# Scaling a normalised block one pass later, and decoding late weights one pass earlier, in a fused delta-rule and gMLP kernel

## The chip, the cores and the metric

The kernel runs on one core of one Trainium2 chip. The metric is the device time of one execution in microseconds (us), lower is better. TensorE is called PE in the profile, VectorE DVE, ScalarE ACT, GpSimd POOL and SyncE SP; SP and POOL issue most of the DMAs here. About 0.5% is what a measurement of this kernel can tell from no change.

## The reference

First a linear-attention recurrence with the delta rule over 768 steps, for 4 batches of 8 heads with a head size of 48; then, on its output, a gated MLP whose gate mixes the tokens of a batch.

```python
for t in range(S):                              # k_n: k with each row divided by its length
    y[:, :, t] = einsum('bhd,bhde->bhe', q[:, :, t], state)
    v_old = einsum('bhde,bhd->bhe', state, kt)
    state = state + bt * einsum('bhd,bhe->bhde', kt, vt - v_old)

h = gelu(x @ w_in)                              # x: y, heads side by side, 384 wide; h: 1024 wide
u, v = h[..., :512], h[..., 512:]
v_n = (v - mean(v)) / sqrt(var(v) + 1e-6) * g_ln
v_s = einsum('ts,bsd->btd', w_sg, v_n) + b_sg[None, :, None]
out = x + (u * v_s) @ w_out
```

## The kernel before, in words

The 768 steps are cut into 12 chunks of 64. The loop over `c` runs 14 passes: in pass c it does chunk c of the recurrence and, as `Ffn(c - 2)`, the first half of the MLP (up to `u` and `v`) for the chunk that ended two passes before. I call the pass by its c. Passes 12 and 13 have MLP work alone. What is left, the mixing of tokens (`spatial`) and the projection (`project`), is the tail, and starts when all chunks are done.

A pass is written as a list of steps, and on every engine the instructions of the loop stand in that order. `turn` transposes the 64 rows of `x` of both batch pairs on PE (L672); ACT copies them, rounded, into `xh` (L673), and DVE subtracts to get the rest, `xl` (L677). A product of two float32 matrices is made of three matmuls with such high and low parts (`mm3`, L650 to L652). `own` and `old` make the chunk's updates, `state` carries the state on, `read` gives the output, and beside them run Gram matmuls for a chunk five passes ahead (passes 0 to 6); all of these are small matmuls of L73. `corner` fills in a part of a triangular inverse for the next chunk: `corner_b` ends with an ACT copy into `z` (L460), which the matmuls beside `read` need. `value` and `gate` are the MLP's matmuls, each closed by an ACT activation (L688 and L720).

`moments` (DVE, L692 and L693) takes mean and variance of `v`. `norm` puts 12 tiny DVE instructions (two columns each: reciprocal square root by Newton steps, L700 to L703) on a list called `slow`, from which `tick` takes one at a time between the larger DVE steps of the inverse (list `bg`), and which `flush` empties. `scale` empties the list and then scales both blocks `vg` on ACT (L711); it is called at the end of the pass, so on ACT it stands between the last copies of this pass and `xh` of the next. `ustore` writes the blocks to memory from POOL's queue in the next pass.

`w_out` and `w_sg` are only needed in the tail. They come in 20 pieces: eight of `w_out`, which are decoded from their stored words in three parts (DVE, then ACT's cast L600, DVE and POOL, then DVE), and twelve of `w_sg`, which are split in two (ACT's cast and a DVE subtraction, L655 and L656). Six buffers `raw` take them as they land; SP issues the load of a piece as soon as its buffer is free. `unit()` stands in seven places of a pass and does one round: part three of one piece, part two of the next, part one of the one after. The pool of these buffers lies where the recurrence's `low` and `prep` pools were, and is opened after pass 9, so rounds run from pass 10 on.

The tail's instructions are written after the loop, and a scheduler places them among the loop's last ones. Its first part loads `vD`, the scaled blocks, into three buffers `vraw` (L1018), from which ACT and DVE make `vnh` and `vnl` (L655 and L656 again).

Of the kernel before, what the change touches and what calls it, by code (L numbers as in the profile page):

```python
# [22 lines left out]
NCH = SEQ // T  # L23
# [15 lines left out]
AHEAD = 5  # L39
# [6 lines left out]
def delta_rule_gmlp_kernel(  # L46
# [14 lines left out]
    nc = tc.nc  # L61
# [93 lines left out]
    bg, slow = [], []  # L155
# [10 lines left out]
    def flush():  # L166
        while slow:
            slow.pop(0)()
# [489 lines left out]
    class Ffn:  # L658
# [46 lines left out]
            self.rs, self.mr = rs, mr  # L705

        def scale(self):
            flush()
            for bi in range(2):
                vg = self.vg[bi]  # L710
                nc.scalar.activation(  # L711
                    out=vg, in_=vg, func=AF.Identity, scale=self.rs[:, bi:bi + 1], bias=self.mr[:, bi:bi + 1])
# [120 lines left out]

    END = {1: (0, "end"), 2: (2, "end"), 3: (4, "end"), 4: (6, "end"), 5: (8, "end")}
    BEGIN = {2: (1, "own"), 3: (3, "own"), 4: (5, "own"), 5: (7, "own")}
    units, stores = [], []
    for c in range(NCH + 2):
        ffn = Ffn(c - 2) if c >= 2 else None
        ch = chain(c) if c < NCH else None
# [6 lines left out]
        def feeds(name, *i):  # L846
            if ffn:
                getattr(ffn, name)(*i)
                if name in COST:
                    spent(name)  # L850
# [6 lines left out]
        def unit():  # L857
            if units:
                units.pop(0)()
# [41 lines left out]
        tload(c + 2)  # L901
        qload(c + 2)
        at("own")
        feeds("value", 0)
        unit()
        does("old0")
        feeds("moments", 0)
        feeds("gate", 0)
        does("old1")
        while stores:  # L910
            stores.pop(0)()
        unit()
        feeds("value", 1)
        does("state0")
        unit()
        feeds("moments", 1)
        feeds("norm")
        feeds("gate", 1)
        at("corner")
        corner(corner_a)  # L920
        does("state1")
        unit()
        if ch:
            gstore(c + AHEAD, nc.sync)
        norms_next()
        feeds("gate", 2)
        unit()
        corner(corner_b)
        feeds("gate", 3)
        unit()  # L930
        if c + AHEAD < NCH and (c + AHEAD) % 2 == 1:
            zload((c + AHEAD) // 2)
        does("read0")
        does("read1")
        at("end")
        unit()
        if ffn:
            ffn.scale()
            stores.append(ffn.ustore)
        if ch:  # L940
            stores.append(lambda c=c: xstore(c))
        if c == NCH - 3:
            prep_ctx.close()
            wpool = ctx.enter_context(tc.tile_pool(name="wpool", bufs=1, side="left", reuse_waits="tile"))
            wouth = wpool.tile([P, ND, DM], F32R, name="wouth")
            woutl = wpool.tile([P, ND, DM], F32R, name="woutl")
            wsgh = wpool.tile([P, NT, SEQ], F32R, name="wsgh")
            wsgl = wpool.tile([P, NT, SEQ], F32R, name="wsgl")
            half = DM // 2
            raws = {}  # L950
            n_w = 2 * (ND + NT)

            def w_fetch(k):
                if k >= n_w:
                    return
                raws[k] = raw = wpool.tile([P, half, 2], I32, name="raw", bufs=6)
                if k < 2 * ND:
                    nc.sync.dma_start(
                        out=raw, in_=words(w_out)[:, k // 2, half * (k % 2):half * (k % 2) + half])
                else:  # L960
                    st, c0 = (k - 2 * ND) // 2, DM * (k % 2)
                    nc.sync.dma_start(
                        out=raw.bitcast(F32).rearrange("p n x -> p (n x)"),
                        in_=w_sgT[st * P:st * P + P, c0:c0 + DM])

            def w_parts(k):

                if k >= n_w:
                    return [lambda: None] * 3
                raw = raws.pop(k)  # L970
                if k < 2 * ND:
                    f = wpool.tile([P, half], I32, name="f", bufs=3)
                    m = wpool.tile([P, half], I32, name="m", bufs=3)
                    cols = slice(half * (k % 2), half * (k % 2) + half)
                    return decode(raw, f, m, wouth[:, k // 2, cols], woutl[:, k // 2, cols])
                st, c0 = (k - 2 * ND) // 2, DM * (k % 2)
                rawf = raw.bitcast(F32).rearrange("p n x -> p (n x)")
                return [lambda: split(wsgh[:, st, c0:c0 + DM], wsgl[:, st, c0:c0 + DM], rawf)] + [lambda: None] * 2

            ahead = []  # L980

            def w_unit(k):
                if k >= 2:
                    ahead[k - 2][2]()
                if k >= 1:
                    ahead[k - 1][1]()
                ahead.append(w_parts(k))
                ahead[k][0]()
                w_fetch(k + 4)

            for k in range(4):
                w_fetch(k)
            units = [lambda k=k: w_unit(k) for k in range(n_w + 2)]
    while units:
        units.pop(0)()
    while stores:
        stores.pop(0)()
    by_hand.close()
# [117 lines left out]
```

## Time and profile before

| | before |
|---|---|
| median of 3 runs | 578.78 us (577.52 to 579.75) |
| the profiled execution, its own time | 572.28 us |
| its span, first to last instruction | 570.6 us |
| PE busy | 462.1 us (81%) |
| DVE busy | 363.9 us (64%) |
| ACT busy | 216.2 us (38%) |
| POOL busy | 98.1 us (17%) |
| mean granted clock of PE | 0.895 |

A row of the timeline gives start and length in us, engine, line, operation, out<-in with sizes, how many were merged, and in brackets the idle time of the engine just before and what ended it. Chains give start, length, engine, tile and line. In a row of the view by stage each engine has its busy time and count, then come the granted clock, the DMA share and GB/s. A busy PE is not PE at its peak, and "issue" is time in which PE waited for nothing that the profile shows. The passes open with their transposes (L672): pass 9 at 307.5 us, 10 at 333.5, 11 at 355.2, 12 at 379.1 and 13 at 399.4; the tail's matmuls begin at 416.7.

### The profile page before, as it was taken

The page shows a single profiled execution, that of the slowest core. Times are in us where ns is not written, and L with a number is a line of the kernel's source. Part 1 is how long each engine was busy: PE and PEld are TensorE (multiplying, and loading weights), DVE is VectorE, ACT ScalarE, POOL GpSimd, SP SyncE. Part 2 cuts the span into 40 slices and gives each one's busy share as a digit, 9 for nine tenths or more (in the row PEclk, how much of TensorE's full clock was granted, in tenths as well). Part 3 has the DMA queues.
Part 4 walks back from the last instruction along what each step waited for, and adds up shares of the span by engine and source line. Part 5 has one row for each costly group of instructions (what it writes and reads, how often), then busy time and mean ns, then how long its engine had stood idle before and what let it go on. Part 6 is the DMA issues. An engine that isn't in the chain of part 4 may idle for free.

```text
span 570.6 us, 18229 instructions
## 1 busy us (share of the span) xinstructions
PE 462.1 (81%) x7635; PEld 416.5 (73%) x7635; DVE 363.9 (64%) x1273; ACT 216.2 (38%) x482; POOL 98.1 (17%) x157
## 2 busy tenths in 40 slices
PE   7244588469796987797998979666599999999997
PEld 5233377357685876686877868556499999999997
DVE  1999799999699649664994338645346545333332
ACT  2212147243763663465547446245343213110110
POOL 3310001320021020102010122301115122211220
PEclk9758858678997987898999999797799999999999
DMA  8798997993699569656954942378449664452113
GB/s 185 171 283 167 214 181 170 184 250 115 121 235 223 199 112 231 163 186 123 257 187 79 266 151 86 107 189 245 140 157 221 168 173 124 118 139 84 43 41 125
DMA packets 153218, 94.35 MB, mean 165 GB/s; under 512 B 117712, under 2 KB 138832, under 8 KB 152176
## 3 DMA queue, kind: packets, MB, share of 16 engines
q1 hardware_dynamic: 137008, 68.84, 51.8%
q0 software_dynamic: 6336, 21.50, 10.5%
q10 hardware_dynamic: 9792, 2.85, 2.8%
q8 instruction: 60, 0.98, 0.8%
q14 instruction: 22, 0.18, 0.1%
HBM read 59.08 MB, written 34.08 MB: 163 GB/s over the span
## 4 chain that ended last, share of the span: by engine, by line
PE 63%; DMA 14%; DVE 9%; issue 5%; ACT 5%; SPq 2%; ACTq 1%; DVEq 0%
PE ps L73 18%; PE ps L650 16%; PE ps L652 14%; PE ps L651 14%; DMA kd<-kqT 3%; DMA vraw<-vD 3%; DMA gd<-gk 2%; DMA z<-zD 2%; DMA zl<-gd 2%; SPq L300 1%; DMA ztd<-zt 1%; ACT vg L711 1%; DMA zD<-zl 1%; DMA kt<-ktok 1%; DVE winl L608 1%
## 5 line engine op out<-in xcount | busy, mean ns | idle before, releaser
L73 PE MATMUL ps<-kd 48*64 48x128 f32 (+1 forms) x896 | 59.7, 292 | 22.7 <-DMA kd<-kqT 20.4
L73 PEld LDWEIGHTS ps<-kd 48*64 48x64 f32 x896 | 52.0, 159 | 25.0 <-issue 20.4
L650 PE MATMUL ps<-winh,xh 128*128 128x512 f32 x72 | 35.4, 491 | 24.9 <-ACT xh L673 20.7
L356 DVE TENSOR_TENSOR ztmp<-zl 128x72 f32<-128x72 f32 (+13 forms) x228 | 52.0, 263 | 1.5
L363 DVE TENSOR_TENSOR zl<-zl,ztmp 128x72 f32<-128x72 f32 (+13 forms) x228 | 50.9, 261 | 0.0
L655 ACT CAST gh<-ga 128x384 fp32r<-128x384 f32 x32 | 16.4, 514 | 90.6 <-POOL ga L1042 90.6
L1042 POOL TENSOR_TENSOR ga<-ga,uT 128x384 f32<-128x384 f32 x32 | 33.7, 1057 | 98.8 <-DVE ga L1040 79.7
L677 DVE TENSOR_TENSOR xl<-ps,xh 128x384 fp32r<-128x384 f32 x24 | 12.3, 552 | 54.8 <-ACT xh L673 54.7
L650 PE MATMUL ps<-xh,winh 128*128 128x256 f32 x144 | 44.5, 309 | 0.0
L73 PE MATMUL ps<-v,z 64*64 64x48 f32 x768 | 31.6, 238 | 14.9 <-issue 14.0
L73 PEld LDWEIGHTS ps<-v,z 64*64 64x64 f32 x768 | 28.6, 153 | 18.7 <-issue 17.3
L651 PE MATMUL ps<-xl,winh 128*128 128x256 f32 x144 | 40.6, 282 | 0.0
L652 PE MATMUL ps<-xh,winl 128*128 128x256 f32 x144 | 40.5, 282 | 0.0
L688 ACT ACTIVATE vg<-ps 128x512 f32<-128x512 f32 x24 | 14.3, 597 | 69.1 <-PE ps L652 67.3
L656 DVE TENSOR_TENSOR gl<-ga,gh 128x384 fp32r<-128x384 f32 x32 | 19.1, 596 | 32.4 <-ACT gh L655 32.4
L515 POOL MEMSET flag<- 1x1 f32 x22 | 2.0, 90 | 218.9 <-PE ps L73 218.9
L650 PEld LDWEIGHTS ps<-winh,xh 128*128 128x128 f32 x72 | 16.0, 222 | 29.7 <-ACT xh L673 21.3
L73 PE MATMUL ps<-s,qo 48*64 48x48 f32 x704 | 27.8, 232 | 6.8 <-issue 6.8
L283 ACT COPY gk<-ps 128x256 f32<-128x256 f32 x40 | 15.0, 376 | 46.0 <-PE ps L73 34.0
L651 PE MATMUL ps<-winl,xh 128*128 128x512 f32 x72 | 32.4, 450 | 0.0
L652 PE MATMUL ps<-wouth,gl 128*128 128x384 f32 x96 | 32.3, 336 | 0.0
L652 PE MATMUL ps<-winh,xl 128*128 128x512 f32 x72 | 32.3, 448 | 0.0
(141 smaller groups left out, 1369.8 us busy)
## 6 DMA issues: line engine op xcount, KB each, us to landing
kd<-kqT SPq DMA_DIRECT2D x20, 384.0 KB, 7.8
vD<-vg POOLq DMA_DIRECT2D x24, 256.0 KB, 4.2
uD<-ut POOLq DMA_DIRECT2D x12, 512.0 KB, 5.7
vraw<-vD SPq DMA_DIRECT2D x48, 128.0 KB, 2.8
uT<-uD SPq DMA_DIRECT2D x32, 192.0 KB, 4.0
gd<-gk SPq DMA_DIRECT2D x11, 512.0 KB, 4.9
z<-zD SPq DMA_DIRECT2D x22, 256.0 KB, 5.5
v<-vtok SPq DMA_DIRECT2D x12, 384.0 KB, 5.4
```

The costliest lines, as they stand in the source:

```text
L73: return nc.tensor.matmul(out=out, lhsT=lhsT, rhs=rhs, start=start, stop=stop, skip_group_check=True)
L283: nc.scalar.copy(out=GK[c % N_M][:, i, :, qd // 2], in_=st["ps"][:, :, 0].rearrange("p j (h t) -> p j h t", h=2))
L356: tv.tensor_tensor(out=st["tmp"][:, at:at + (r1 - r0) * w].rearrange("p (r t) -> p r t", t=w), in0=z[:, r0:r1, i:i + 1].broadcast_to([P, r ...
L363: tv.tensor_tensor(out=z[:, r0:r1, i + 1:32], in0=z[:, r0:r1, i + 1:32], in1=st["tmp"][:, at:at + (r1 - r0) * w].rearrange("p (r t) -> p r ...
L650: nc.tensor.matmul(out=ps, lhsT=sh, rhs=mh, start=(first and i == 0), stop=False)
L651: nc.tensor.matmul(out=ps, lhsT=sh, rhs=ml, start=False, stop=False)
L652: nc.tensor.matmul(out=ps, lhsT=sl, rhs=mh, start=False, stop=(last and i == n - 1))
L655: nc.scalar.copy(out=hi, in_=src)
L656: nc.vector.tensor_tensor(out=lo, in0=src, in1=hi.bitcast(F32), op=ALU.subtract)
L677: nc.vector.tensor_tensor(out=self.xl[:, :, bi], in0=srcs[bi], in1=self.xh[:, :, bi].bitcast(F32), op=ALU.subtract)
L688: nc.scalar.activation(out=vg, in_=ps, func=AF.Gelu_apprx_tanh)
L1042: nc.gpsimd.tensor_tensor(out=ga, in0=ga, in1=uT[:, d], op=ALU.mult)
```

## The change

Three things are written in another order; no instruction of the computation is added or removed.

First, `scale` no longer empties `slow`, and is not called at the end of its pass: it is put on a list `scales`, which the next pass empties behind its first `value`. Second, `slow` is emptied at the end of the pass as before, and also ahead of the unit behind `gate` 2 if `bg` is empty. Third, the block that closes `prep_ctx`, opens `wpool` and defines the pieces moves from the end of pass 9 to before its first `value`, with three empty rounds ahead, so that the first four rounds fall in the second half of pass 9.

```diff
         def scale(self):
-            flush()
             for bi in range(2):
                 vg = self.vg[bi]
                 nc.scalar.activation(
...
-    units, stores = [], []
+    units, stores, scales = [], [], []
     for c in range(NCH + 2):
...
         at("own")
+        if c == NCH - 3:
+            prep_ctx.close()
+            wpool = ctx.enter_context(tc.tile_pool(name="wpool", bufs=1, side="left", reuse_waits="tile"))
...
+            def w_unit(k):
+                if k >= 2:
+                    ahead[k - 2][2]()
+                if k >= 1:
+                    ahead[k - 1][1]()
+                ahead.append(w_parts(k))
+                ahead[k][0]()
+                w_fetch(k + 4)
+
+            for k in range(4):
+                w_fetch(k)
+            units = [lambda: None] * 3 + [lambda k=k: w_unit(k) for k in range(n_w + 2)]
         feeds("value", 0)
+        while scales:
+            scales.pop(0)()
         unit()
...
         feeds("gate", 2)
+        if not bg:
+            flush()
         unit()
...
         at("end")
         unit()
         if ffn:
-            ffn.scale()
+            flush()
+            scales.append(ffn.scale)
             stores.append(ffn.ustore)
...
-        if c == NCH - 3:
-            prep_ctx.close()
...
-            units = [lambda k=k: w_unit(k) for k in range(n_w + 2)]
     while units:
         units.pop(0)()
+    while scales:
+        scales.pop(0)()
     while stores:
         stores.pop(0)()
```

How this moves instructions on ACT and SP is seen in three places. The first is ACT at the end of pass 9 and the start of pass 10, from the last activation of `gate` (`ut`). Before:

```order
L460 COPY z_106<-ps 32x8x2x32 x2
L720 ACTIVATE ut<-ps 128x256
L563 COPY x_5273<-ps 128x384
L478 COPY w_108<-ps 128x512
L563 COPY x_5309<-ps 128x384
L478 COPY w_108<-ps 128x512
L711 ACTIVATE vg<-vg,mr,rsq_y 128x512 x2
L673 CAST xh<-ps 128x3x128 x2
L688 ACTIVATE vg<-ps 128x512
```

And with the change:

```order
L600 CAST wouth<-f 128x192
L460 COPY z_106<-ps 32x8x2x32 x2
L719 ACTIVATE ut<-ps 128x256
L600 CAST wouth<-f 128x192
L563 COPY x_5336<-ps 128x384
L478 COPY w_108<-ps 128x512
L563 COPY x_5372<-ps 128x384
L478 COPY w_108<-ps 128x512
L600 CAST wouth<-f 128x192
L673 CAST xh<-ps 128x3x128 x2
L688 ACTIVATE vg<-ps 128x512
L710 ACTIVATE vg<-vg,mr,rsq_y 128x512 x2
```

Three casts of `w_out` pieces now stand here, one of them ahead of the copy into `z`, and the scaling has gone behind the activation of `value`.

The second place is ACT at the start of pass 12, behind the last copies of the recurrence (`x`). Before:

```order
L563 COPY x_6079<-ps 128x384
L655 CAST wsgh<-raw 128x384
L655 CAST vnh<-vraw 128x512
L711 ACTIVATE vg<-vg,mr,rsq_y 128x512 x2
L673 CAST xh<-ps 128x3x128 x2
L655 CAST vnh<-vraw 128x512 x3
L688 ACTIVATE vg<-ps 128x512
```

And with the change:

```order
L563 COPY x_6105<-ps 128x384
L655 CAST wsgh<-raw 128x384
L673 CAST xh<-ps 128x3x128 x2
L655 CAST vnh<-vraw 128x512
L688 ACTIVATE vg<-ps 128x512
L710 ACTIVATE vg<-vg,mr,rsq_y 128x512 x2
L655 CAST wsgh<-raw 128x384
```

The first cast of the tail (`vnh`) and the scaling stood ahead of `xh`, and are now behind it.

The third place is SP's queue, from the first piece's load to the tail's first loads. Before:

```order
L958 DMA raw<-w_out 128x384 x8
L962 DMA raw<-w_sgT 128x384 x11
L1003 DMA g_sb<-g_ln 128x4x1
L1004 DMA bsg_bc<-b_sg 128x768
L1018 DMA vraw<-vD_75 64x512
L962 DMA raw<-w_sgT 128x384
L1018 DMA vraw<-vD_75 64x512 x5
```

And with the change:

```order
L919 DMA raw<-w_out 128x384 x8
L923 DMA raw<-w_sgT 128x384 x12
L1009 DMA g_sb<-g_ln 128x4x1
L1010 DMA bsg_bc<-b_sg 128x768
L1024 DMA vraw<-vD_75 64x512 x6
```

One load of `w_sg` has moved ahead of the tail's loads, and nothing else.

More of the change, by code (lines that the diff above doesn't have):

```diff
@@ L903, in delta_rule_gmlp_kernel @@
         at("own")
[L904 to L937, printed above, removed]
-            ffn.scale()
-            stores.append(ffn.ustore)
-        if ch:
-            stores.append(lambda c=c: xstore(c))
         if c == NCH - 3:
@@ L992, in delta_rule_gmlp_kernel @@
                 w_fetch(k)
-            units = [lambda k=k: w_unit(k) for k in range(n_w + 2)]
+            units = [lambda: None] * 3 + [lambda k=k: w_unit(k) for k in range(n_w + 2)]
+        feeds("value", 0)
+        while scales:
+            scales.pop(0)()
+        unit()
+        does("old0")
+        feeds("moments", 0)
+        feeds("gate", 0)
+        does("old1")
+        while stores:
+            stores.pop(0)()
+        unit()
+        feeds("value", 1)
+        does("state0")
+        unit()
+        feeds("moments", 1)
+        feeds("norm")
+        feeds("gate", 1)
+        at("corner")
+        corner(corner_a)
+        does("state1")
+        unit()
+        if ch:
+            gstore(c + AHEAD, nc.sync)
+        norms_next()
+        feeds("gate", 2)
+        if not bg:
+            flush()
+        unit()
+        corner(corner_b)
+        feeds("gate", 3)
+        unit()
+        if c + AHEAD < NCH and (c + AHEAD) % 2 == 1:
+            zload((c + AHEAD) // 2)
+        does("read0")
+        does("read1")
+        at("end")
+        unit()
+        if ffn:
+            flush()
+            scales.append(ffn.scale)
+            stores.append(ffn.ustore)
+        if ch:
+            stores.append(lambda c=c: xstore(c))
     while units:
         units.pop(0)()
+    while scales:
+        scales.pop(0)()
     while stores:
```

## The prediction

> **What bounds the kernel now.** I read the chain of waits first, in order of time; its last lines are these (start, length, what).
>
> ```profile
> 363.62 0.80 PE ps L650
> ...
> 381.31 5.58 DMA vraw<-vD
> 386.97 0.63 ACT vnh L655
> ...
> 405.67 0.80 ACT vg L711
> 406.89 0.79 PE ps L650
> ```
>
> From 406.89 us on the chain is TensorE alone. Three times before that, TensorE's first `value` matmul (L650) comes behind a ScalarE instruction that it does not need: the scaling of the previous blocks (L711) or a cast for the tail (`vnh`). I call these matmuls V11, V12 and V13, after the passes c = 11, 12, 13, and the transposes that open a pass T11, T12, T13. The view by stage has the reads that end pass 10, then a row from each T to its V, and for two of them the matmuls behind (stretch, length, busy time and count of PE, PEld, DVE, ACT, POOL, then granted clock, DMA share, GB/s):
>
> ```profile
> 352.80:355.20 2.40, 2.40 (x132) 2.20 (x131) 2.19 (x8) 1.95 (x5) 0.53 (x1) 1.00 0.30 85
> 355.20:363.62 8.42, 3.20 (x137) 2.78 (x135) 5.76 (x26) 3.28 (x8) 1.55 (x4) 0.92 0.19 51
> 363.62:367.00 3.38, 3.38 (x8) 2.71 (x9) 3.17 (x10) 0.32 (x1) 1.01 (x2) 0.50 0.15 40
> 379.13:389.42 10.29, 0.88 (x10) 0.64 (x6) 3.12 (x15) 3.34 (x7) 0.68 (x2) 0.67 0.76 182
> 389.42:393.00 3.58, 3.58 (x9) 2.83 (x10) 2.21 (x4) 1.64 (x4) 2.02 (x4) 0.51 0.90 305
> 399.41:406.89 7.48, 0.82 (x9) 0.58 (x7) 3.68 (x16) 3.92 (x9) 0.66 (x2) 0.75 0.13 38
> 430.00:566.80 136.80, 136.76 (x789) 136.44 (x787) 59.32 (x102) 23.33 (x45) 33.68 (x32) 1.00 0.48 125
> ```
>
> T12 to V12 is 10.29 us with 0.88 us of matmuls, T13 to V13 7.48 with 0.82. After the first two waits the clock is about 0.50 for some 3.4 us, so a cooling costs 3.4 x 0.5 = 1.7 us more; I take the third alike. The last row is the tail: no gap, full clock. So whatever brings V13 forward comes off the end. The timeline of ScalarE and the waits say what is late:
>
> ```profile
> 361.69 1.52 ACT L711 ACTIVATE vg<-vg,mr,rsq_y 128x512 f32<-128x512 f32 x2 [4.65 <-DVE mr L703]
> 379.62 0.51 ACT L655 CAST wsgh<-raw 128x384 fp32r<-128x384 f32 x1
> 386.97 0.62 ACT L655 CAST vnh<-vraw 128x512 fp32r<-128x512 f32 x1 [6.83 <-DMA vraw<-vD]
> ACT wouth L600 <- DVE f L596: 0.9, 2, 0.5
> ```
>
> **The end of the recurrence, T12 to the tail.** The change takes L711 out from between T and `xh`, and in the new order pass 12's `xh` stands ahead of the first `vnh`. What then lies between T12 and V12 is one weight cast (379.62 + 0.51 = 380.13), `xh` and the split behind it: about 1.7 us for 10.29, gain 8.6. At T13 four `vnh` casts still stand ahead of `xh`; the fourth needs a load whose buffer the first frees. When do these loads start?
>
> ```profile
> 374.06 0.60 ACT L688 ACTIVATE vg<-ps 128x512 f32<-128x512 f32 x1 [1.12 <-PE ps L652]
> 378.06 0.56 DVE L656 TENSOR_TENSOR wsgl<-raw,wsgh 128x384 fp32r<-128x384 f32 x1 [0.50 <-ACT wsgh L655]
> 379.02 0.43 SPq L1003 DMA_DIRECT2D g_sb<-g_ln  x1
> ```
>
> SP's queue holds its last weight loads until a `raw` buffer comes free, that is until the piece six before is split (378.62, then `g_sb` at once). Afterwards the split that frees the last of them follows the second `value` of pass 11, whose activation (374.06) now lies 10.4 us behind V11, 8.7 without the cooling; with cast and split some 10 us. So `vraw` starts some 11 us behind V11 (near 375) and lands by 381 at the 5.6 us of the chain's row. The first `vnh` then ends by 382, as the matmuls of `value` in pass 12 do, and the fourth by 386 to 389, around T13. I take 2.0 us from T13 to V13 (1.7 if it is there, 3.5 if not): gain 5.5. Three coolings less: 3 x 1.7 = 5.1. Sum **19.2 us**, if V11 stays where it is.
>
> **Passes 9 to 11: the cost.** Eight pieces of `w_out` are decoded in 2.70 us of VectorE each (from one L590 to the next below). Now they start in pass 9, where VectorE stood idle for 11.56 us.
>
> ```profile
> 336.32 1.02 DVE L677 TENSOR_TENSOR xl<-ps,xh 128x384 fp32r<-128x384 f32 x2 [11.56 <-ACT xh L673]
> 339.27 0.25 DVE L590 TENSOR_SCALAR m<-raw 128x192 int32<-128x192 int32 x1
> 352.45 0.25 DVE L590 TENSOR_SCALAR m<-raw 128x192 int32<-128x192 int32 x1
> 355.15 0.25 DVE L590 TENSOR_SCALAR m<-raw 128x192 int32<-128x192 int32 x1
> 359.27 0.16 DVE L700 TENSOR_SCALAR ve<-mv 128x2 f32<-128x2 f32 x1
> 361.43 0.16 DVE L703 SCALAR_TENSOR_TENSOR mr<-mv,rsq_y 128x2 f32<-128x2 f32 x1
> L958 SPq DMA_DIRECT2D raw<-w_out x1: 420/420/420, 323.8 to 323.8; - x1
> DMA to landing us min/median/max: 5.4/5.4/5.4
> 327.18 1.18 ACT L460 COPY z<-ps 32x512 f32<-32x512 f32 x2 [0.64 <-PE ps L73]
> 333.08 0.26 PE L73 MATMUL ps<-u,m 64*64 64x48 f32 x2 [2.83 <-issue]
> 356.68 0.35 ACT L600 CAST wouth<-f 128x192 fp32r<-128x192 f32 x1 [0.49 <-DVE f L596]
> ```
>
> SP's order is unchanged, so opening the pool sooner loads nothing sooner: the first piece lands at 323.8 + 5.4 = 329.2. ScalarE's first cast (L600) now stands ahead of the `z` copy L460, and needs VectorE's first part of that piece (about 1.5 us): 330.7, so the copy ends near 332.2 instead of 328.36, and behind it wait `x`, `w` and TensorE's reads. Of these 3.8 us, 2.83 lie over the stall at 333.08 that is there now ("issue"): T10 about 1 us late. VectorE goes on: norm 2.3 (359.27 to 361.59), then up to the fourth piece three rounds less a last part, 3 x 2.7 - 0.7 = 7.4; so 329.2 + 1.5 + 2.3 + 7.4 = 340.4, and with a split of 0.55 V10 is at 341.0. Now it ends an `xl` pair begun at 336.32 and V10 is at 337.66: **3.3 us late**. In pass 10 VectorE has `xl`, `v`, `m` (336.32 to 339.27: 2.95), four rounds (10.8) and two moments (1.8): 356.0 for the eighth piece. Its cast, one weight cast and the `z` copy again stand in line: 0.35 + 0.51 + 1.18 give 358.0. Reads take 2.4 (352.80:355.20), and T11 to the end of `own` 3.76 (8.42 less the wait of 4.66 named below): V11 at 358.0 + 2.4 + 3.8 = 364.2 against 363.62. So V11 is **0.6 us late** in place of being earlier: the wait for `mr` at 361.69 is gone, and the same VectorE work has been paid before. Bounds: 3 us earlier (TensorE alone from V10, were it not late), 5 us later (each of the two `z` copies and V10 lets TensorE cool, 3 x 1.7).
>
> ```profile
> 363.62 0.80 PE L650 MATMUL ps<-winh,xh 128*128 128x512 f32 x1 [4.66 <-ACT xh L673]
> 238.00 0.26 PE L73 MATMUL ps<-v,z 64*64 64x48 f32 x2 [3.24 <-issue]
> 239.46 0.79 PE L650 MATMUL ps<-winh,xh 128*128 128x512 f32 x1
> ```
>
> A wait of 3.24 us was already followed by slow matmuls (0.79, as at 363.62). The new waits before V10 and at the copy are of 3.6 and 3.8 us; at V10 the loss of 1.7 mostly hides behind VectorE, which sets the next `z` copy, so I add nothing. The Trainium skill speaks against the change here: "TensorE: Matmul & The Clock Gate", section "What's actually happening", says that about 3.4 us without work, in a window that runs freely, brings half clock, and as long a busy stretch restores it. By it both new waits may cool: my time plus up to 3.4 us. The trace agrees on half clock and the 3.4 us; that 3.24 us sufficed, a free window allows.
>
> **Passes 3 to 9: small terms.** L711 also leaves its place ahead of `xh` here, and goes ahead of the copies behind `value`.
>
> ```profile
> 155.57 0.49 PE L650 MATMUL ps<-winh,xh 128*128 128x512 f32 x1 [0.69 <-DVE xl L677]
> 207.38 0.51 PE L650 MATMUL ps<-winh,xh 128*128 128x512 f32 x1 [0.99 <-DVE xl L677]
> 265.58 0.50 PE L650 MATMUL ps<-winh,xh 128*128 128x512 f32 x1 [0.66 <-DVE xl L677]
> 312.82 0.50 PE L650 MATMUL ps<-winh,xh 128*128 128x512 f32 x1 [0.51 <-DVE xl L677]
> 187.23 0.37 ACT L283 COPY gk<-ps 128x256 f32<-128x256 f32 x1 [0.45 <-PE ps L73]
> 187.50 0.38 ACT L285 COPY m<-ps 128x256 f32<-128x256 f32 x1
> 188.44 1.06 PE ps L73 x32
> ```
>
> Gain: four waits for `xl`, 2.85 us. Loss: in the four passes with Gram work (3 to 6) the copy of `m` ends at 187.88, 0.56 us before the next matmuls at 188.44; two scalings (1.52) less the idle 0.45 push it 1.07, so 0.5 past, four times: 2.0. Bounds: +2.85 if that bank is not the one needed, and, at 1.52 in each of passes 3 to 11, -13.7 + 2.85 = -10.8. I take +0.8, nearest to the rows. Stores wait for the later scaling by 3 to 4 us; POOL's queue holds nothing else that TensorE needs before the next pass. The steps put ahead at `not bg` move only in passes 9 and later.
>
> **Sum.** 19.2 - 0.6 + 0.8 = 19.4 us off the profiled execution's own 572.28 (span 570.6): 552.9. The median of the runs shown is 578.78, 6.5 us above that execution; I carry the same 6.5: **559.4 us**.
>
> **Rivals.**
> (a) The casts hold ScalarE longer in passes 9 to 11 than reckoned: V11 5 us late and no gain in passes 3 to 9: 19.2 - 5 = 14.2, so 564.6. For it: each cast waits for a VectorE part, with TensorE's copies behind. Against: ScalarE waited 0.9 us for such parts in all. Chance 0.17.
> (b) T13 stays held by the fourth `vnh`: 5.5 and one cooling of 1.7 are not gained: 566.6. For it: its load comes behind a buffer and others in SP's queue, at a DMA share of 0.90 (389.42:393.00). Chance 0.13.
> (c) The change doesn't do what it says: loads come no sooner and `vnh` follows as now, so ScalarE's `value` and `gate` work of pass 12 queues behind 386.97, and V13 gains only what T12's order gives, some 3 us: 576. Against: the `raw` buffers come free by VectorE's pace, which moves. Chance 0.07.
> (d) Slower: the pieces' casts become the bound. If each of the eight casts of `wouth` held TensorE for its whole VectorE round and let it cool half the time, 8 x (2.70 + 0.85) = 28.4 us against 19.4: 587.8. It decides from 2.4 us a cast. For it: passes 9 and 10 put all eight ahead of copies. Against: TensorE has work in its queue under most of them. Chance 0.05.
> The forecast keeps 0.58; its own range is 554 to 564. From (a) and (b) the range goes up to 571, and down to 551 with the better bounds (V11 3 us earlier, +2 in the middle): **551 to 571**. About 0.5% (2.9 us) is what can be told from no change: faster 0.88, same 0.06, slower 0.06.
>
> **What would show it.** In the changed profile: T12 to V12 under 2.5 us and T13 to V13 under 4; granted clock 1.00 behind V12 and V13; V13 16 us earlier or more; the `z` copies of passes 9 and 10 ended 3 us late with L600 waiting for VectorE ahead of them; V10 late by about 3 us; no stall before `value` of the odd passes below 9. Wrong it would be if V11 came more than 5 us late, if `xh` of pass 13 still waited for `vraw`, or if the tail were no longer at full clock.

## The result, and the profile after

The changed kernel takes 560.52 us in the median of four runs (557.59 to 561.25), the kernel before 579.26 on the same chip: a ratio of 0.974, 95% interval 0.970 to 0.978, so 18.7 us or 2.6% less. The forecast was 559.4. Run again on another occasion the ratio was 0.966 (0.960 to 0.972).

The profiled execution after took 560.41 us (span 558.7), the one before 572.28 (span 570.6). These two differ by 11.9 us only, since the profile before was of an execution 7.0 us below this median (the prediction, with one run less, carried 6.5). Executions of one and the same kernel differ by 2% and more (the kernel before: 568.75 to 582.46 us in a series of 13), mostly ahead of pass 9 (experiment 1). The ratios compare fast executions alone, while the profiles of units_only, norm_late, raw_first and three are of executions 1.8 to 2.4% above the fastest of their kernel. So I read both traces from T9 on, the transposes that open pass 9, to S, the first matmul of the tail's `spatial`. From S to the end every kernel here takes 153.8 to 154.9 us.

The view by stage of the changed kernel: first the two stretches T9 to T11 and T11 to S, then shorter ones inside them (stretch, length, busy time and count of PE, PEld, DVE, ACT, POOL, then granted clock, DMA share, GB/s).

```profile
311.44:363.79 52.35, 44.37 (x1018) 38.48 (x1016) 32.55 (x104) 26.84 (x60) 10.97 (x22) 0.93 0.54 156
363.79:404.23 40.44, 36.99 (x439) 32.18 (x437) 22.25 (x69) 23.33 (x51) 7.71 (x16) 0.96 0.71 213
...
335.39:339.60 4.21, 4.08 (x125) 3.77 (x125) 3.79 (x16) 1.81 (x5) 0.71 (x1) 0.50 0.01 4
...
344.61:348.00 3.39, 3.39 (x42) 2.67 (x42) 3.25 (x7) 0.96 (x2) 0.00 (x0) 1.00 0.01 2
...
367.99:381.01 13.02, 13.02 (x182) 11.55 (x182) 5.53 (x21) 7.79 (x17) 2.80 (x6) 1.00 0.62 198
381.01:382.45 1.44, 0.88 (x10) 0.64 (x6) 1.39 (x4) 1.32 (x4) 0.00 (x0) 1.00 0.86 248
382.45:391.19 8.74, 8.74 (x54) 7.65 (x55) 5.42 (x12) 6.70 (x14) 2.68 (x5) 1.00 0.81 217
391.19:392.25 1.06, 0.82 (x9) 0.58 (x7) 0.96 (x5) 0.86 (x3) 0.00 (x0) 1.00 1.11 388
392.25:394.62 2.37, 0.73 (x2) 0.29 (x2) 2.06 (x12) 0.33 (x1) 0.00 (x0) 1.00 1.11 346
394.62:398.60 3.98, 3.98 (x13) 3.37 (x14) 0.41 (x1) 0.52 (x1) 0.00 (x0) 0.57 0.64 163
```

T12 to V12 is 1.44 us (10.29 before), T13 to V13 is 1.06 (7.48 before), and from V11 to T13 the clock is at 1.00, where it was at half behind V11 and V12. Behind V13 it falls to 0.57 once more. The timeline of PE shows which waits are left in these passes.

```profile
335.39 0.96 PE L73 MATMUL ps<-z,kt 64*64 64x64 f32 x3 [4.34 <-ACT z L460]
...
344.61 0.50 PE L650 MATMUL ps<-winh,xh 128*128 128x512 f32 x1 [1.70 <-DVE xl L677]
...
361.19 0.33 PE L73 MATMUL ps<-z,kt 64*64 64x64 f32 x2 [0.78 <-ACT z L460]
...
382.45 0.51 PE L650 MATMUL ps<-winh,xh 128*128 128x512 f32 x1 [0.56 <-ACT xh L673]
...
392.25 0.51 PE L650 MATMUL ps<-winh,xh 128*128 128x512 f32 x1 [0.24 <-ACT xh L673]
...
394.62 0.50 PE L652 MATMUL ps<-winh,xl 128*128 128x512 f32 x1 [1.65 <-DVE xl L677]
...
404.23 0.34 PE L650 MATMUL ps<-wsgh,vnh 128*128 128x384 f32 x1
```

Three waits of over 1 us are new: 4.34 us for the `z` copy of pass 9, 1.70 us for `xl` ahead of V10, which the prediction had (V10 late), and 1.65 us for `xl` at the third matmul of V13. The causes of the first and the last stand in the timelines of DVE, ACT and SP.

```profile
333.27 0.26 DVE L590 TENSOR_SCALAR m<-raw 128x192 int32<-128x192 int32 x1 [8.41 <-DMA raw<-w_out]
334.51 0.35 ACT L600 CAST wouth<-f 128x192 fp32r<-128x192 f32 x1 [5.56 <-DVE f L596]
334.77 1.17 ACT L460 COPY z<-ps 32x512 f32<-32x512 f32 x2
...
359.50 0.36 DVE L596 SCALAR_TENSOR_TENSOR f<-m,f 128x192 f32<-128x192 f32 x1
360.56 1.17 ACT L460 COPY z<-ps 32x512 f32<-32x512 f32 x2
...
379.01 3.69 SPq L1024 DMA_DIRECT2D vraw<-vD  x6
384.50 0.62 ACT L655 CAST vnh<-vraw 128x512 fp32r<-128x512 f32 x1 [1.71 <-DMA vraw<-vD]
...
389.96 0.62 ACT L655 CAST vnh<-vraw 128x512 fp32r<-128x512 f32 x1
...
391.71 0.86 ACT L673 CAST xh<-ps 128x384 fp32r<-128x384 f32 x2
391.77 0.17 DVE L700 TENSOR_SCALAR ve<-mv 128x2 f32<-128x2 f32 x1
394.02 1.01 DVE L677 TENSOR_TENSOR xl<-ps,xh 128x384 fp32r<-128x384 f32 x2
```

In pass 9 the first piece lands at 333.2, its cast waits for it, and the `z` copy stands behind the cast. In pass 13 `xh` begins at 391.71, but DVE first runs the 12 small norm steps of pass 12 (391.77 to 394.0), and only then `xl`.

### The profile page after: what moved, and what is told of

It is laid out like the page before. It is cut to its first block, busy times and chain, and to the rows that moved or that the text cites. A ratio compares the mean times of both kernels' runs of the same rounds, so it can differ in the third digit from the quotient of the medians.

```text
span 558.7 us, 18235 instructions
## 1 busy us (share of the span) xinstructions
PE 460.9 (82%) x7634; PEld 415.5 (74%) x7635; DVE 362.8 (65%) x1273; ACT 214.0 (38%) x482; POOL 98.6 (18%) x157
## 3 DMA queue, kind: packets, MB, share of 16 engines
q0 software_dynamic: 6336, 21.50, 10.8%
q10 hardware_dynamic: 9792, 2.85, 2.9%
## 4 chain that ended last, share of the span: by engine, by line
PE 38%; DMA 11%; DVE 6%; issue 4%; ACT 2%; SPq 1%; POOL 0%; DVEq 0%; ACTq 0%; POOLq 0%
PE ps L650 10%; PE ps L652 10%; PE ps L651 10%; PE ps L73 7%; DMA z<-zD 3%; DMA vraw<-vD 3%; DMA zD<-zl 2%; DMA raw<-w_out 1%; DMA xD<-x 1%; DVE f L594 1%; DMA gd<-gk 1%; DVE bs L692 1%; PE ps L672 1%; SPq L300 1%; DVE f L596 1%
## 5 line engine op out<-in xcount | busy, mean ns | idle before, releaser
L73 PE MATMUL ps<-kd 48*64 48x128 f32 (+1 forms) x896 | 59.4, 289 | 24.7 <-DMA kd<-kqT 20.8
L363 DVE TENSOR_TENSOR zl<-zl,ztmp 128x72 f32<-128x72 f32 (+13 forms) x228 | 50.8, 261 | 0.0
L73 PE MATMUL ps<-v,z 64*64 64x48 f32 x768 | 31.1, 236 | 10.5 <-issue 9.6
L656 DVE TENSOR_TENSOR gl<-ga,gh 128x384 fp32r<-128x384 f32 x32 | 18.7, 584 | 31.9 <-ACT gh L655 31.9
L73 PEld LDWEIGHTS ps<-v,z 64*64 64x64 f32 x768 | 28.2, 151 | 13.9 <-issue 12.5
L650 PE MATMUL ps<-winh,xh 128*128 128x512 f32 x72 | 33.1, 460 | 5.7 <-DVE xl L677 4.8
L73 PE MATMUL ps<-z,gk 32*64 32x64 f32 x384 | 17.1, 250 | 24.8 <-DMA z<-zD 24.8
L73 PEld LDWEIGHTS ps<-z,gk 32*64 32x64 f32 x384 | 15.3, 161 | 26.8 <-issue 25.9
L73 PE MATMUL ps<-z,kt 64*64 64x64 f32 x704 | 27.3, 229 | 7.4 <-ACT z L460 7.3
L650 PE MATMUL ps<-wsgh,vnh 128*128 128x384 f32 x96 | 32.4, 337 | 0.4 <-ACT vnh L655 0.4
```

Of the source, the lines that this page charges most:

```text
L73: return nc.tensor.matmul(out=out, lhsT=lhsT, rhs=rhs, start=start, stop=stop, skip_group_check=True)
L363: tv.tensor_tensor(out=z[:, r0:r1, i + 1:32], in0=z[:, r0:r1, i + 1:32], in1=st["tmp"][:, at:at + (r1 - r0) * w].rearrange("p (r t) -> p r ...
L650: nc.tensor.matmul(out=ps, lhsT=sh, rhs=mh, start=(first and i == 0), stop=False)
L656: nc.vector.tensor_tensor(out=lo, in0=src, in1=hi.bitcast(F32), op=ALU.subtract)
```

## The experiments

All kernels compute the whole result. Ratios are to the kernel before on the same chip, with the 95% interval, which reaches 0.4 to 1.1% to each side; the 0.5% named above for what can be told from no change is too small for most of them. The two stretches, taken from one profile each, say more than the ratio about what an edit does; how far they repeat is seen in the two kernels that were profiled twice.

| kernel | T9 to T11 | T11 to S | T9 to S | ratio of time |
|---|---|---|---|---|
| before | 47.7 | 61.5 | 109.2 | 1 |
| before_again | 47.0 | 64.1 | 111.2 | 1 |
| scale_only | 47.8 | 50.8 | 98.5 | 0.974 (0.967 to 0.980) |
| units_only | 56.9 | 54.2 | 111.1 | 1.001 (0.995 to 1.007) |
| after | 52.4 | 40.4 | 92.8 | 0.974 (0.970 to 0.978) |
| after_again | 52.7 | 38.4 | 91.1 | 0.966 (0.960 to 0.972) |
| norm_late | 52.3 | 41.9 | 94.2 | 0.965 (0.953 to 0.976) |
| flush_12 | 53.0 | 37.1 | 90.0 | 0.959 (0.950 to 0.968) |
| skip_slot | 49.5 | 39.4 | 88.9 | 0.963 (0.956 to 0.970) |
| raw_first | 49.4 | 41.5 | 90.9 | 0.960 (0.952 to 0.968) |
| raw_flush | 48.8 | 37.2 | 86.0 | 0.958 (0.953 to 0.964) |
| three | 48.8 | 40.5 | 89.3 | 0.958 (0.951 to 0.965) |
| xl_first | 50.6 | 37.2 | 87.8 | 0.958 (0.953 to 0.964) |
| scale_xl | 46.2 | 44.7 | 90.8 | 0.959 (0.954 to 0.965) |

### 1. Where executions differ: the same kernels once more

No edit in either.

> The kernel before, profiled once more. The profile shown of it took 572.28 us, below every one of its other runs (577.5 to 579.9). Theory: the 6.5 us that this execution lacked lie in waits for transfers ahead of pass 9 (matmuls on `z` waiting for `z<-zD`, stalls called issue), so that an execution of 577 to 580 us shows T9 at 310 to 314 us instead of 307.5, and from T9 on the same lengths as before within 1 us (T9 to V11 56.1, V11 to the first spatial matmul 53.1, from there to the end 153.9). Rival: the 6.5 us lie behind T9, in the waits that the change removes; then T9 to V11 or V11 to the first spatial matmul is 4 us or more longer than shown, and part of the measured gain comes from there.

> The changed kernel once more, on the same chip as the two below. Theory: what differs between executions of one kernel lies ahead of T9; T9 to the first spatial matmul is 92 to 95 us again (92.8 in the profile shown), V11 to there 36 to 38, and the time 3% below the kernel before, as at first. Rival: the stretch behind T9 varies as well, by 3 us or more, and the differences of a few us read from one profile each (scale_only 98.5, flush_12 90.0, skip_slot 88.9) are not told from chance.

before_again took 579.33 us (span 577.6), 7.0 us more than the profile shown of before. Its T9 comes at 312.62 in place of 307.51, its T9 to S is 111.2 in place of 109.2, the rest to the end 153.82 in place of 153.87. So 5.1 of the 7.0 us lie ahead of pass 9, which the theory had, and 2 behind it, where the theory allowed 1 us in each stretch: T9 to V11 is 55.4 (56.1), but V11 to S 55.7 (53.1). after_again had T9 at 309.41 in place of 311.44, and 91.1 in place of 92.8 behind it (92 to 95 expected; V11 to S 34.7, 36 to 38 expected). Over all 14 profiles T9 lies between 302.4 and 316.0, with no order by kernel that I can see. In these two pairs the stretch T9 to S repeats within 2 us; smaller differences in the table's fourth column are not told from chance, and the rival of after_again (3 us or more) is not borne out.

### 2. The scaling's place alone

```diff
         def scale(self):
-            flush()
...
         feeds("value", 0)
+        while scales:
+            scales.pop(0)()
...
         if ffn:
-            ffn.scale()
+            flush()
+            scales.append(ffn.scale)
```

> Of the change only the scaling's move behind the next pass's first `value`; the pool is opened and the pieces decoded as before, from pass 10 on. In this order `xh` of pass 12 stands ahead of the first `vnh`, four `vnh` ahead of `xh` of pass 13. Theory of the prediction (the scaling's place frees T12, sooner pieces are what frees T13): V11 loses its wait of 4.66 us and comes 2 to 4 us sooner, T12 to V12 under 2.5 us, but V13 still waits for the fourth `vnh`, whose load is held by the weights' buffers, by 4 us or more; the time falls by 12 to 15 us. Rival: the scaling's place alone does it all, since the buffers come free by the pace of the passes, which moves as well: T13 to V13 under 3 us and the time 17 us or more below before, the sooner pieces being worth nothing.

The view by stage (T9 to T11, T11 to S) and PE's timeline:

```profile
307.12:354.87 47.75, 42.70 (x1019) 37.21 (x1017) 22.96 (x67) 25.45 (x55) 8.47 (x18) 0.96 0.59 162
354.87:405.62 50.75, 38.72 (x438) 33.06 (x437) 32.47 (x105) 25.17 (x56) 9.90 (x19) 0.90 0.62 189
```

```profile
361.77 0.50 PE L652 MATMUL ps<-winh,xl 128*128 128x512 f32 x1 [2.56 <-DVE xl L677]
...
375.76 0.50 PE L650 MATMUL ps<-winh,xh 128*128 128x512 f32 x1 [0.56 <-ACT xh L673]
...
391.81 0.80 PE L650 MATMUL ps<-winh,xh 128*128 128x512 f32 x1 [4.39 <-ACT xh L673]
```

And ACT's, from the first `vnh` to `xh` of pass 13:

```profile
381.98 0.62 ACT L655 CAST vnh<-vraw 128x512 fp32r<-128x512 f32 x1 [5.89 <-DMA vraw<-vD]
...
391.24 0.89 ACT L673 CAST xh<-ps 128x384 fp32r<-128x384 f32 x2
```

T12 to V12 is 1.44 us (374.32 to 375.76), V13 still waits 4.39 us, and T9 to S falls by 12 us against the mean of the two profiles before. The ratio gives 15 us of 576. (It is not the fourth `vnh` itself that V13 waits for: that ends at 387.74. The first `vnh` waited 5.89 us for its load, and `xh` comes last of the activations and casts that had queued up on ACT behind it.) So the theory's split holds for the waits: the scaling frees T12, not T13. It is also by far the larger part of the gain: T11 to S loses 12.1 us of 62.8, and T9 to T11 nothing.

### 3. The sooner pieces alone

The third part of the change without the first two: the pool is opened and the pieces decoded from pass 9's second half on, `scale` (with `flush` in it) at the end of its pass.

> Of the change only the pool and the pieces: opened in pass 9, decoded from its second half on; the scaling at the end of its pass as before, with the norm's steps ahead of it. Here the first `vnh` stands ahead of `xh` of pass 12, and three more ahead of that of pass 13. Theory: pass 9 loses some 2 to 4 us as in the changed kernel, the wait for `mr` ahead of V11 stays in part, V12 waits for the first `vraw` until some 385 to 387 us, 2 to 5 us behind T12, and V13 comes some 6 to 9 us sooner than before: the time falls by 5 to 10 us. Rival: without the scaling's move nothing is gained, because `xh` is queued behind the same chain; within 3 us of before.

```profile
316.04:372.90 56.86, 47.46 (x1019) 41.11 (x1017) 32.63 (x94) 27.41 (x60) 11.55 (x22) 0.88 0.54 153
372.90:427.11 54.21, 41.90 (x439) 36.36 (x437) 23.95 (x76) 25.25 (x52) 7.18 (x15) 0.81 0.57 170
```

```profile
348.52 1.52 ACT L711 ACTIVATE vg<-vg,mr,rsq_y 128x512 f32<-128x512 f32 x2 [3.58 <-DVE mr L703]
...
351.05 0.80 PE L650 MATMUL ps<-winh,xh 128*128 128x512 f32 x1 [4.47 <-DVE xl L677]
...
400.43 0.79 PE L650 MATMUL ps<-winh,xh 128*128 128x512 f32 x1 [5.00 <-ACT xh L673]
```

No gain: the ratio is 1.001, T9 to S as before. The theory expected 5 to 10 us and was wrong, its rival is right in number. The stages show why it is not nothing that happened: some 9 us of DVE work moved from the second stretch to the first (23.1 to 32.6 busy, 32.5 to 24.0). The second gained 8.6 us against the mean before, and the first lost 9.5. There the pieces stand on DVE ahead of the norm's steps, so `mr` comes late, the scaling on ACT waits 3.58 us for it, `xh` stands behind the scaling, and V10 waits 4.47 us. The scaling at the pass's end makes PE wait for whatever DVE has in front of `mr`; moving pieces in front of it moves the wait to pass 10.

Put together, experiments 2 and 3 tell more than each: the pieces cost 4.8 us in T9 to T11 with the scaling moved (52.5, the mean of the two profiles after, against 47.8) and 9.5 without; they gain 11.3 in T11 to S with it (39.4 against 50.8) and 8.6 without. Worth 6.5 us on top of the scaling, nothing without it. (The 6.5 holds the second part of the change too; without that part, in norm_late, it is 4.3.) In the ratio of time that 6.5 us (1.1%) does not show clearly: 0.974 for scale_only against 0.974 and 0.966.

### 4. The norm's steps put ahead

The changed kernel without the two lines `if not bg: flush()`.

> The changed kernel without the norm's steps put ahead in passes 9 and later (they come at the end of the pass again). Theory: they stand ahead of the next `xl` on VectorE either way, and the casts of the pieces need only the first part of a piece: within 1.5 us of the changed kernel. Rival: the 2.3 us of small steps at the pass's end come between the last piece and `xl` and hold V10 and V11: 2 to 5 us slower than the changed kernel.

T9 to S is 94.2 against 92.8 and 91.1 (within 1.5 us expected), the ratio 0.965. By the time it is no different, and the stretch does not tell the theory from its rival; by the trace the wait for `xl` that stood in pass 13 is now in pass 12:

```profile
387.91 0.79 PE L652 MATMUL ps<-winh,xl 128*128 128x512 f32 x1 [2.19 <-DVE xl L677]
```

and pass 13 has none. The second part of the change by itself does nothing that can be measured; it chooses where the 2.3 us of small steps stand in front of an `xl`.

### 5. The new waits, one by one

Three kernels take away new waits of the changed kernel: skip_slot and raw_first that of pass 9, each by another means, flush_12 that of pass 13.

skip_slot leaves the unit's slot ahead of `corner_b` of pass 9 empty and lets two pieces of `w_sg` share one later:

```diff
-            units = [lambda: None] * 3 + [lambda k=k: w_unit(k) for k in range(n_w + 2)]
+            todo = [lambda k=k: w_unit(k) for k in range(n_w + 2)]
+            both = lambda: (todo[11](), todo[12]())
+            units = [lambda: None] * 3 + todo[:1] + [lambda: None] + todo[1:11] + [both] + todo[13:]
```

> The changed kernel with the slot ahead of corner_b of pass 9 left empty, so that the first cast of a piece (L600) stands behind the `z` copy L460 there and every later piece one slot later, until two pieces of `w_sgT` share a slot in pass 11; the end of the decoding stays where it is. Theory: the wait of 4.34 us at the `z` copy of pass 9 goes, one round of 2.7 us less stands ahead of `xl` of pass 10, V10 comes about 3 us and V11 2 to 3 us sooner (T9 to V11 54 us). Rival: VectorE has the same work to do by V11 either way, so V11 stays (56 to 57 us) and the wait in pass 9 was free.

raw_first moves the block that opens the pool and issues the first loads from behind to ahead of these lines of pass 9:

```diff
+        if c == NCH - 3:
+            prep_ctx.close()
...
         vload(c + 2)
         tload(c + 2)
         qload(c + 2)
         at("own")
```

> The changed kernel with one thing moved: in pass 9 the pool is opened and the first four `raw` loads are issued ahead of that pass's loads of `v`, `kt` and `qo` in SP's queue, which stood 5.4 us before them (320.99 to 326.37). Theory: the decoding on VectorE, which runs without a gap from the landing of the first piece (333.2) to `xl` of pass 11, sets V10 and V11; with the landing some 5 us sooner the wait of 4.34 us at the `z` copy of pass 9 falls under 2, and T9 to V11 falls from 56.5 to 50 to 53 us; from there to the first spatial matmul 36 us as in the changed kernel. Rival: the landing only moves the wait, to stalls called issue and to the copies, and TensorE's own work sets V11; T9 to V11 stays within 1.5 us of 56.5. Second rival: the loads wait for the memory of the closed pools and land no sooner.

flush_12 leaves pass 12's norm steps on the list until `turn` of pass 13 is issued:

```diff
         feeds("turn")
+        if c == NCH + 1:
+            flush()
...
-        if not bg:
+        if not bg and c != NCH:
             flush()
...
         if ffn:
-            flush()
+            if c != NCH:
+                flush()
             scales.append(ffn.scale)
```

> The changed kernel with the small norm steps of pass 12 (2.3 us of VectorE from 391.77) behind `xl` of pass 13 in place of ahead of it; `turn` then finds none of them to run. Theory: the wait of 1.65 us for `xl` ahead of the third `value` matmul of pass 13 falls under 0.5, and with it the half clock behind it (0.63 and 0.51 from 394.6 to 398.6): from V13 to the first spatial matmul 9 us or less in place of 11.98. Rival: the clock falls there for another reason (the short work of the transposes), or `vnl` splits take the place of the norm steps: 11 us or more.

Each did what its theory said to the wait. In skip_slot the 4.34 us at the `z` copy are gone, T10 follows T9 by 23.7 us (28.2 in the changed kernel), and T9 to V11 is 54.3 (304.33 to 358.63; expected 54): its rival, that the wait was free, falls, since the three kernels with the changed order up to there (after, after_again, flush_12) give 56.4 to 56.9. V10 still waits:

```profile
327.67 0.26 PE L73 MATMUL ps<-u,m 64*64 64x48 f32 x2 [2.10 <-issue]
...
334.66 0.80 PE L650 MATMUL ps<-winh,xh 128*128 128x512 f32 x1 [2.89 <-DVE xl L677]
```

In raw_first the first load is issued 10.7 us behind T9 in place of 14.9, and the first piece is there 18.3 behind it in place of 21.8; the wait at the `z` copy is 0.41. T9 to V11 is 53.4, just outside the 50 to 53 expected, but 3 us less than in the changed kernel. What it gave there came back in part at the end (T11 to S 41.5), with V13 now waiting for `xh` as well as for `xl`:

```profile
334.09 0.32 PE L73 MATMUL ps<-z,kt 64*64 64x64 f32 x2 [0.41 <-ACT z L460]
...
392.28 0.50 PE L650 MATMUL ps<-winh,xh 128*128 128x512 f32 x1 [1.36 <-ACT xh L673]
...
395.01 0.79 PE L652 MATMUL ps<-winh,xl 128*128 128x512 f32 x1 [2.00 <-DVE xl L677]
```

In flush_12 no wait for `xl` over 0.3 us is left at V13, and from V13 to S it takes 8.84 us (387.66 to 396.50) in place of 11.98. (Four of the 12 steps still stand ahead of `xl`, because `turn` itself runs that many; the expectation had said none.) The three rows are of flush_12 from T13 on, the fourth is of after_again behind its wait for `xl`:

```profile
386.60:387.66 1.06, 0.82 (x9) 0.58 (x7) 0.96 (x5) 0.86 (x3) 0.00 (x0) 1.00 1.03 396
387.66:390.00 2.34, 2.26 (x9) 1.57 (x10) 2.10 (x11) 0.33 (x1) 0.00 (x0) 1.00 1.09 371
390.00:392.00 2.00, 2.00 (x15) 1.82 (x14) 1.16 (x4) 1.57 (x3) 0.00 (x0) 1.00 1.01 253
...
392.50:396.50 4.00, 4.00 (x22) 3.47 (x23) 1.72 (x4) 1.99 (x4) 0.00 (x0) 1.00 0.45 130
```

The clock is 1.00 in all four, where the changed kernel's profile has 0.57. Not all of the 3.1 us is thereby settled as the edit's: the second profile of the changed kernel had the wait too (1.76 us) and kept the clock at 1.00, and there V13 to S was 10.5 us. So I put the wait at some 1.7 us, and the half clock that may or may not follow at 1.5 more; both are differences of single profiles.

### 6. Edits together

raw_flush is raw_first with flush_12; three adds the empty slot of skip_slot; xl_first is three with the norm's steps behind the next `xl` in every pass from 9 on (`if not bg: flush()` behind `turn`, none ahead of it, and no `tick` inside it there). In fact that edit reaches earlier passes too, wherever `bg` is empty at `turn`: in passes 5 and 7 of xl_first the last norm steps (`mr`, 215.15 and 268.17 us) come behind `xl` (213.64 and 266.65). This lies ahead of T9.

> Both: the loads of the pieces sooner and the norm steps of pass 12 behind `xl`. Theory: the two gains add, 4 to 6 us and 3 us; T9 to the first spatial matmul 84 to 87 us in place of 92.8, and the time 7 to 9 us below the changed kernel, near 552. Rival: with V11 sooner, the `vraw` loads do not come sooner by as much and `vnh` holds T13 again: T9 to the first spatial matmul 89 us or more.

> Three edits on the changed kernel together: loads of the pieces sooner, the slot ahead of corner_b of pass 9 empty, and the norm steps of pass 12 behind `xl` (all but the four that `turn` itself runs). Theory: the waits that the single edits removed are different ones, so V10 loses its wait of 2.1 us that the two-edit kernel still has, and T9 to the first spatial matmul falls to 83 to 85 us (86.0 with two edits, 92.8 without). Rival: TensorE's own work between V10 and V11 is the floor, and the empty slot adds nothing to the sooner loads: 85.5 to 87.

> As three, and in every pass from 9 on the norm's steps (2.3 us of VectorE) come behind the next pass's `xl`, all twelve of them. Theory: nothing but pieces is then ahead of `xl` of passes 10 and 11, V10 and V11 come 1 to 2 us sooner than in three, T9 to the first spatial matmul 81.5 to 84 us; the scaling, behind the first `value`, does not wait. Rival: the steps push the pieces instead, which the next `z` copy waits for, or the scaling waits for `mr` and holds ScalarE: the same as three or up to 3 us more.

raw_flush has T9 to S in 86.0 us (84 to 87 expected), 6 us under the mean of the changed kernel; its time, 550.46 us in the median of six, is 4.2% under the kernel before (expected: near 552). Its ratio, 0.958, lies below both of the changed kernel (0.974 and 0.966), but its interval overlaps that of the second, so by the time alone the step beyond the change is not settled. The other two give the same ratio, and longer stretches, 89.3 and 87.8, where 83 to 85 and 81.5 to 84 were expected. Both theories were wrong. In both, the wait at V10 was gone, as they said, but PE's own stalls at the end of pass 9 were longer, and V13 waited 1.1 us for `xh`. In three the 3.3 us over raw_flush lie behind T11, in xl_first the 1.8 ahead of it. These rows are of three:

```profile
338.63 0.26 PE L73 MATMUL ps<-u,m 64*64 64x48 f32 x2 [4.82 <-issue]
...
392.69 0.50 PE L650 MATMUL ps<-winh,xh 128*128 128x512 f32 x1 [1.14 <-ACT xh L673]
```

In raw_flush the stall called issue at the same place is 0.57, in xl_first 2.65, in before 2.83. What sets its length is open. Nothing here tells the three kernels apart in time.

### 7. Late pieces with the norm out of the way

The last one asks whether the sooner pieces are needed at all: scale_only with the norm's steps behind the next `xl` from pass 9 on (and, as in xl_first, wherever `bg` is empty at `turn`; `turn` itself runs no step there).

```diff
         feeds("turn")
+        if not bg:
+            flush()
...
         if ffn:
-            ffn.scale()
+            if bg:
+                flush()
+            scales.append(ffn.scale)
```

> The kernel before with the scaling behind the next `value`, as in scale_only, and the norm's steps behind the next `xl` in passes 9 and later; pool and pieces as before, from pass 10 on. It removes from scale_only its waits of 2.56 us (`xl`, V11) and 2.19 us (`xl`, pass 12) and leaves its wait of 4.39 us for `xh` ahead of V13, which stands behind four `vnh`. Theory: the pieces' place is worth something by itself, because with pass 13 sooner the `vraw` transfers hold V13 the longer: T13 to V13 6 us or more, T9 to the first spatial matmul 94 to 97 us (98.5 in scale_only, 92.0 in the mean of the changed kernel's two profiles). Rival: the loads move with the passes and the order of `xl` replaces the sooner pieces: T13 to V13 under 4 us, T9 to the first spatial matmul 92 us or less, the time at or below the changed kernel's (0.966 to 0.974 of before).

```profile
302.41:348.56 46.15, 41.51 (x1019) 36.10 (x1017) 23.35 (x71) 25.34 (x55) 8.55 (x18) 1.00 0.61 170
348.56:393.22 44.66, 36.83 (x439) 31.63 (x437) 31.18 (x102) 24.73 (x56) 10.10 (x19) 0.92 0.67 197
```

```profile
374.26 0.62 ACT L655 CAST vnh<-vraw 128x512 fp32r<-128x512 f32 x1 [6.52 <-DMA vraw<-vD]
...
383.18 0.79 PE L650 MATMUL ps<-winh,xh 128*128 128x512 f32 x1 [6.35 <-ACT xh L673]
```

The theory was right about the wait: T13 to V13 is 7.17 us, as `vraw` holds the casts ahead of `xh` of pass 13 (ACT works off its queue behind the first of them, as in scale_only). It was wrong about the sum: T9 to S is 90.8, not 94 to 97, and the ratio is 0.959. Against scale_only T9 to T13 got shorter by 5.9 us and V13 to S by 3.8, while T13 to V13 grew by 2.0. So with the small steps behind `xl`, pieces left where they were are as good as the change, in time and in T9 to S. The pieces' place decides in the first place where the time goes: to T9 to T11 (50.6 in xl_first, 46.2 here) or to V13 (T11 to S 37.2 and 44.7). Whether sooner pieces still gain something then is not shown: xl_first is 3.0 us shorter from T9 to S but has sooner loads and an empty slot besides, and its ratio is the same (0.958); the change with this one edit alone was not run.

## Why the prediction was right, and where it was not

The time was right within 1.1 us, the size by median (19.4 expected, 18.7 measured) too. That closeness is in part luck. The interval of the ratio is 5 us wide, and the second measurement gives 19.6 us. In the two profiles shown T9 to S is 16.4 us shorter where the steps below add up to 18.6 (18.2 in the mean of two profiles each), and what lies ahead of T9 varies by up to 13.6 us. By its steps, each counted from T9 or V11, since T9 itself was 3.9 us later in the profile after:

- **Passes 9 to 11.** The `z` copy of pass 9 was to end 24.7 us behind T9 and ended at 24.5 (335.94); V10 3.3 us late, measured 3.0; VectorE's part of the eighth piece at 48.5, measured 48.4 (359.86); the `z` copy of pass 10 at 50.5, measured 50.3; V11 0.6 us later than before, measured 0.4 (56.5 against 56.1). One part was off: T10 was to be 1 us late and was 2.2, because the wait of 4.34 us brought half clock (0.50 over the 125 small matmuls of 335.39 to 339.60). The prediction had named that cost and left it out as hidden behind VectorE, which then set V10: so it was (V10 waited 1.70 us for `xl` all the same). Rival (a), V11 5 us late, did not come true.
- **T12.** 1.7 us forecast, 1.44 measured; the cause was `xh` ahead of the first `vnh`, which scale_only shows by itself.
- **T13.** The loads of `vraw` were to start 11 us behind V11 and did (379.01 against 367.92: 11.1; before, 381.31 against 363.62: 17.7). The fourth `vnh` ended at 390.58, 0.6 us ahead of T13, so rival (b) did not come true, but by little: in raw_first, with passes sooner by some 3 us, the fourth `vnh` waited for its load and V13 1.36 us for `xh`, and in scale_xl the queue behind the first `vnh` held V13 by far longer. The 2.0 us forecast from T13 to V13 was 1.06. The step that failed in this part is that I took `xh` for the last thing V13 waits for. `xl` needs VectorE, and there `flush` of pass 12 put 12 small steps ahead of it: 1.65 us.
- **The three coolings.** Before, there were three, as the sum had it (the third, for which it showed no row: 0.54 over 406.89 to 410.30). Those behind V11 and V12 are gone, that behind V13 is not (0.57 over 394.62 to 398.60); the sum had 1.7 us for it. With the wait for `xl`, V11 to S came out at 36.3 us where 33.9 was forecast, so the end gained 16.8 us in this profile for 19.2; 34.7 us in the second profile, where the clock held. The Trainium skill's "TensorE: Matmul & The Clock Gate", section "What's actually happening", gives half clock after at least one idle window of some 3.4 us, and lets that window run freely. The trace does not agree with the first: 1.65 us of waiting was enough in one profile (0.57), and 1.76 us was not in the other (1.00). Nor does a wait of 3.24 us, which the prediction laid to a free window, fill one of 3.4. That the free run of the window decides between two like waits would fit, but no run here shows it.
- **Passes 3 to 9.** +0.8 forecast. From T3 to T9 the three profiles with the old scaling take 157.3, 157.8 and 160.8 us, the eleven with the new one 151.6 to 161.4, on average 156.8. A gain of 0.8 can be neither seen nor excluded; a loss near the 10.8 of the bounds, which count passes 3 to 11, is not there. The two parts of the term can be read singly. The gain is larger than the 2.85 us forecast: T to V, summed over passes 3, 5, 7 and 9, is 21.2 to 21.3 us in all three profiles with the old scaling, 15.6 and 17.3 in the two of the changed kernel. The loss of 2.0 us for late copies is not seen: in passes 3 to 8 of those two profiles PE has no wait for ACT of 0.2 us or more. So both parts were mis-sized, on the safe side, and the rest of these passes scatters by more.
- **What the gain is owed to.** The prediction gave T12 to the scaling and T13 to the sooner pieces, and that is where the waits went. It did not say that the pieces are worth nothing without the scaling (units_only), nor that another order of the same small steps gives the same without them (scale_xl). Rival (c), that the loads come no sooner, fell with the 11.1 us for 17.7; (d) fell, as eight casts cost T9 to T11 4.8 us and not 28.
- **The range.** Its lower end does not come out of its bounds: V11 3 us early in place of 0.6 late and 2 more in passes 3 to 9 take 559.4 to 553.7, not 551; the upper end, 571, is the sum of (a) and (b).

## What to carry to other kernels

When an engine's queue holds an instruction that waits for a slow chain elsewhere (here the scaling, for `mr`), first move that instruction behind the work it does not concern; until then work moved in front of the chain only moves the wait. Then look at every operand of the first stalled matmul: the cast was freed and the subtraction behind it, on another engine, was what PE waited for next, behind 2.3 us of tiny steps. And when executions differ by more ahead of the stretch in which the change acts than the change is worth, as here ahead of pass 9, compare the traces from there on.

## What the runs showed that I had not expected

- Ahead of pass 9, where these kernels differ little, T9 still lies anywhere between 302.4 and 316.0 us. From pass 2 on, the waits that come and go there are mainly of two kinds: PE for `z<-zD` (up to 5.1 us in a pass; ahead of pass 2 it is 5.9 to 9.1 in every profile) and stalls called issue (up to 5.4).
- The length of a wait does not settle by itself whether half clock follows. Between T9 and S, PE's clock fell to 0.50 to 0.58 behind every wait or stall of 2.89 us or more. Below that it went either way: 0.57 behind 1.65 us (changed kernel, V13), 0.58 behind 1.49 (raw_first, V10), but 1.00 behind 1.76 (after_again, V13), 1.70 (changed kernel, V10) and 2.56 (scale_only, V11). What decides there is open.
- At the end of pass 9 a stall called issue and the wait for the `z` copy just ahead of it take each other's place: no such stall behind waits of 2.48 to 4.82 us (units_only, norm_late, flush_12 and both profiles of the changed kernel), 1.18 behind 0.41 (raw_first), 0.57 behind 0.70 (raw_flush), and 2.10 to 4.82 where PE does not wait for `z` (2.10 in skip_slot, 2.83 before, 4.82 in three). So part of a removed wait can come back under another name, by an amount that nothing here predicts.
